# Transposing all tiles of the second round through DRAM, in eight parts, and four early groups in place of five

## The chip, the cores and the metric

One core of a Trainium2 chip. The metric is the device time of one launch in microseconds; medians of several runs are given.

## The reference

Attention with keys that are pooled 4x4, then a two-layer network with a sigmoid-approximated Gelu, over 49152 tokens of 128 channels:

```python
kv_flat = kv.reshape(B, H//4, 4, W//4, 4, C).mean(axis=(2, 4)).reshape(B, -1, C) @ w_sr   # 768 keys a batch
a = softmax((q @ kv_flat.T) / sqrt(C));  x = (a @ kv_flat).reshape(B * S, 128)            # B=4, S=12288
h = x @ w_in                                        # 128 -> 2048
out = (h * (1 / (1 + exp(-1.702 * h)))) @ w_out     # 2048 -> 128
```

## The kernel before

A Python program lays out a static order for every engine. The 96 groups of 512 queries are done in two rounds of 48: attention, network, attention, network. Attention needs Exp, the network Gelu, so each stage change costs ScalarE a table load (1.28 us in the trace). ScalarE handles three chunks of 512 columns in one activation of 128x1536; two sets of three PSUM banks alternate. Two more banks serve as accumulators and scratch. `ag`, 102 slots of 512 columns, holds activations until TensorE drains them. (A fill is a matmul that writes the banks that an activation will read; a drain is a matmul that reads an activation's result.)

The network needs attention's output with channels on partitions, so each 128x128 tile must be transposed. In both rounds the first 72 tiles (`LATER`) are turned on TensorE, six at a time, and copied back by VectorE; the other 120 go through DRAM in six parts of 20, during the network.

Five "early" groups of round two are worked during network 1: TensorE makes the scores and VectorE computes the exponentials with a polynomial, which spares ScalarE 10 activations.

```python
EARLY = 5
...
def drain_attn(t, a):                       # attention times value of tile t, half of the keys
    ...
        nc.tensor.matmul(av_of[u][...], weights(("a", i, jc))[:, o:o + T], vs[...], ...)
    ...
        o = u * TS % (XS * SG // T)
        if o >= LATER:
            to = x[:, o * T:(o + TS) * T]...
        else:                                # to be turned on TensorE: into a small tile first
            if u % 2 == 0:
                xt_of[u // 2] = npool.tile([128, 2 * TS, C], BF, name="xt")
            to = xt_of[u // 2][:, u % 2 * TS:u % 2 * TS + TS, :]
        nc.vector.tensor_tensor(to, ps[:, :, 0:C], rec..., MUL)
        if u % 2 and o < LATER:
            turns.append((now + TURN, u // 2))
...
def turn(w):
    for k in range(n):                       # n = 6
        nc.tensor.transpose(ps[:, k, :], xt[:, k, :], ident)
    nc.vector.tensor_copy(x[:, o:o + n * T], ps...)
...
LATER, PART = 72, 20
def put_away(n, m):  nc.sync.dma_start(out=x_bf[...], in_=x[:, ...])            # PART tiles
def bring_back(n, m): nc.sync.dma_start_transpose(out=x[:, ...], in_=x_bf[...])
...
def background_moe(g):
    n, g = divmod(g, 4 * XS)
    m, odd = divmod(g - 9, 2)
    if 0 <= m < (4 * XS * G // T - LATER) // PART:
        (bring_back if odd else put_away)(n, m)
...
def fill_moe(chunks, ps):                    # 3 matmuls, then one activation of 128x1536
def drain_moe(g, fc):                        # one matmul of a 16-step accumulation; VectorE evacuates
...
# the order's own estimates, in units of one 512-column matmul
FIXED, CHUNK, SWITCH, HANDOVER, EVACUATE, LATE = 0.33, 1.975, 6.0, 1.0, 4.5, 1.0
```

The softmax here doesn't subtract the row's maximum and nothing guards it: scores larger than these inputs give would overflow.

Of the kernel before, what the change touches and what calls it, by code (L numbers as in the profile page):

```python
# [24 lines left out]
def kernel(  # L25
# [12 lines left out]
    G = 512  # L38
    SG = 4 * G
# [5 lines left out]
    T = 128  # L45
    TS = 3
# [11 lines left out]

    R = 2
    XS = NS // R  # L60
    EARLY = 5
    AG = 102

    cpool = ctx.enter_context(tc.tile_pool(name="const", bufs=1))
# [19 lines left out]
    def acc(key=None):  # L84

        nonlocal last_acc
        last_acc = next_acc()
        if key:
            closes[last_acc] = key
        return banks[:, last_acc, :]  # L90
# [7 lines left out]
    def close(key, then):  # L98
        for m in [m for m in closes if closes[m] == key]:
            del closes[m]  # L100
            free[m] = then
# [59 lines left out]
    def add_kv(b, n):  # L161
        i, w = divmod(n, r)
        if n == 0:
            kv_sums[b] = kvsum.tile([Hp, 2, Wp, C], F32, name="kvs")
        for i2 in range(2):
            nc.gpsimd.dma_start(out=kv_sums[b][:, i2], in_=kv_p[b, i, w, :, i2],  # L166
                                **({"accum_op": ADD} if n else {}))
# [147 lines left out]

    early = range(NG // R, NG // R + EARLY)

    def weights(c):
        if c[0] == "a" and c[1] in early:
            return ag[:, (c[1] - early[0]) * JC + c[2], :]  # L320
        return ag[:, slot_of[c], :]
# [11 lines left out]
    def drain_attn(t, a):  # L333

        i, u, k = t // 4, t // TS, t % TS
        if k == a == 0:
            av_of[u] = acc(("av", u))
        o = t % 4 * T
        for jc in range(a * K, a * K + K):
            nc.tensor.matmul(av_of[u][:, k * (C + 1):(k + 1) * (C + 1)], weights(("a", i, jc))[:, o:o + T],  # L340
                             vs[i // GB][:, jc, 0:C + 1], start=(jc == 0), stop=(jc == JC - 1))
            if t % 4 == 3 and i not in early:
                del slot_of["a", i, jc]
        if k == TS - 1 and a == 1:
            close(("av", u), max(now, dve - 1.0) + EVACUATE)
            on_dve(4.3)
            ps = av_of.pop(u)[:, 0:TS * (C + 1)].rearrange("p (k c) -> p k c", k=TS)
            rec = npool.tile([128, TS], F32, name="rec")
            nc.vector.reciprocal(rec, ps[:, :, C])  # L349
            o = u * TS % (XS * SG // T)  # L350
            if o >= LATER:
                to = x[:, o * T:(o + TS) * T].rearrange("p (k c) -> p k c", k=TS)
            else:
                if u % 2 == 0:
                    xt_of[u // 2] = npool.tile([128, 2 * TS, C], BF, name="xt")
                to = xt_of[u // 2][:, u % 2 * TS:u % 2 * TS + TS, :]
            nc.vector.tensor_tensor(to, ps[:, :, 0:C], rec.unsqueeze(2).broadcast_to([128, TS, C]), MUL)  # L357
            if u % 2 and o < LATER:
                turns.append((now + TURN, u // 2))


    LN2 = 0.6931471805599453
# [51 lines left out]
        nc.vector.tensor_copy(x[:, o:o + n * T], ps.rearrange("p k t -> p (k t)"))  # L414


    LATER, PART = 72, 20

    def put_away(n, m):
        o = LATER + m * PART  # L420
        lo = n * XS * SG + o * T
        nc.sync.dma_start(out=x_bf[lo:lo + PART * T, :].rearrange("(k p) c -> p k c", p=T),
                          in_=x[:, o * T:(o + PART) * T].rearrange("p (k c) -> p k c", k=PART))

    def bring_back(n, m):
        o = LATER + m * PART
        lo = n * XS * SG + o * T
        nc.sync.dma_start_transpose(out=x[:, o * T:(o + PART) * T].unsqueeze(1), in_=x_bf[lo:lo + PART * T, :])

# [3 lines left out]
    def gate():  # L433

        nc.vector.memset(gate_tile, 0.0)  # L435
        nc.gpsimd.memset(gate_tile, 0.0)  # L436
# [3 lines left out]
    def background(i):  # L440

        s = i // 4
        if i % 4 == 0:
            if QS <= s + 2 < NS:
                load_qT(s + 2)
            if CAST <= s + CAST < NS:
                gate()
                cast_q(s + CAST)
        if i == 10:
            gate()  # L450
            for jc in range(JC):
                load_chunk(1, jc)
        if 0 <= i - 16 < JC:
            extras.append((key_and_value, 1, i - 16))
        if 0 <= i - 15 < JC:
            extras.append((pool_chunk, 1, i - 15))
        if i == 26:
            gate()
            nc.gpsimd.dma_start(out=w_in_sb, in_=moe_w_in)
        if i == 34:  # L460
            gate()
            nc.gpsimd.dma_start(out=w_out_sb, in_=moe_w_out.rearrange("(o p) c -> p o c", p=128))

    def background_moe(g):

        n, g = divmod(g, 4 * XS)
        m, odd = divmod(g - 9, 2)
        if 0 <= m < (4 * XS * G // T - LATER) // PART:
            (bring_back if odd else put_away)(n, m)
        g += n * 4 * XS  # L470
        nonlocal head, low
        if g == 12:
            low = EARLY * JC
            head = max(head, low)
        if g in (40, 46):
            i = early[0] + 4 * (g // 46)
            begun.add(("a", i))
            background(i)
        for b, lo in ((2, 2), (3, 24)):
            if lo <= g < lo + 8:  # L480
                gate()
                add_kv(b, g - lo)
            if g in (lo + 10, lo + 12):
                use_kv(b, (g - lo - 10) // 2)

    def use_kv(b, a):
        nonlocal extra_at
        sum_kv(b, a)
        on_dve(3.5)
        extra_at = max(extra_at, dve + 1.5)  # L490
        extras.extend([(transpose_pooled, b, a), (make_k, b, a), (make_v, b, a)])
# [38 lines left out]
    for n in range(R):  # L530
        part = [c for c in chunks if c[0] // (NG // R) == n]
        while part:
            m = sizes.pop(0) if sizes else K
# [21 lines left out]
    def prepare(p):  # L555

        nonlocal now
        for f, *args in first.get(p, ()):
            if f in COST:
                now = max(now, free[next_acc()])  # L560
            f(*args)
            if f in COST:
                now += COST[f][0]
                free[last_acc] = now + COST[f][1]
        kind, part = seq[p]
        for i, _ in part:
            if (kind, i) not in begun:
                begun.add((kind, i))
                (background if kind == "a" else background_moe)(i)
# [32 lines left out]
    def on_dve(cost):  # L602
        nonlocal dve
        dve = max(dve, now + 1.0) + cost
# [114 lines left out]
```

## Time and profile before

| | before |
|---|---|
| time, median of 3 runs | 974.97 us (974.95 to 976.67) |
| span of the profiled run | 974.7 us |
| first network activation | 150.28 us |
| network 1, first activation to the first of attention 2 | 354.49 us |
| attention 2, to the first activation of network 2 | 118.62 us |
| network 2, first to last activation | 343.65 us |

The last four rows are read from the starts of ScalarE's activations in the trace. One pair of profile lines is wanted here beside those of the prediction: the summary of the chain that ended last.

```profile
PE 91%; ACT 4%; DMA 3%; DVE 1%; issue 0%; POOL 0%; ACTq 0%; POOLq 0%
```

### The profile page before, as it was taken

How to read it: one execution, taken by the hardware profiler on the slowest of the kernel's cores; microseconds unless marked ns; L12 is line 12 of the kernel's file. 1: busy time of each engine (PE TensorE's matmuls, PEld its weight loads, DVE VectorE, ACT ScalarE, POOL GpSimd, SP SyncE). 2: the span in 40 equal slices, each digit the busy share in tenths (PEclk: the TensorE clock that was granted, in tenths of full speed). 3: DMA queues.
4: the chain of work that ended last, by engine and by line, in shares of the span. 5: the costliest groups of instructions: out<-in, count | busy, mean ns of one | idle time of the engine just before them, and what ended most of it. 6: DMA issues, size and time to landing. Idle time of an engine off the chain costs nothing.

```text
span 974.7 us, 16041 instructions
## 1 busy us (share of the span) xinstructions
PE 956.3 (98%) x6431; PEld 513.2 (53%) x6431; DVE 385.6 (40%) x806; ACT 945.0 (97%) x703; POOL 65.8 (7%) x113
## 2 busy tenths in 40 slices
PE   7899999999999999999999999999999999999997
PEld 3567777644444444444445777764444444444443
DVE  4444333211477878788786443330110110110110
ACT  4999999999999999989999999999999999999997
POOL 3100100430000232000000000000000000000000
PEclk9999999999999999999999999999999999999999
DMA  9897861999564798215257520002567522222222
GB/s 182 160 196 145 115 95 34 110 165 159 115 139 67 107 148 110 41 28 82 33 87 136 115 45 23 2 1 44 120 119 137 112 34 44 44 33 44 44 33 44
DMA packets 335691, 85.01 MB, mean 87 GB/s; under 512 B 309568, under 2 KB 333248, under 8 KB 335296
## 3 DMA queue, kind: packets, MB, share of 16 engines
q1 hardware_dynamic: 305456, 51.34, 31.0%
q0 software_dynamic: 29104, 32.51, 22.1%
q8 instruction: 50, 0.82, 0.3%
q10 hardware_dynamic: 1056, 0.13, 0.1%
q14 instruction: 25, 0.20, 0.1%
HBM read 52.49 MB, written 43.52 MB: 98 GB/s over the span
## 4 chain that ended last, share of the span: by engine, by line
PE 91%; ACT 4%; DMA 3%; DVE 1%; issue 0%; POOL 0%; ACTq 0%; POOLq 0%
PE banks L500 33%; PE banks L507 33%; PE banks L340 13%; PE banks L329 11%; ACT ag L502 3%; DMA qT<-q_bf 2%; ACT ag L331 1%; DMA x<-in_q_dram 1%; PE banks L412 1%; PE banks L370 1%; DVE qT L230 1%; PE banks L224 0%; DVE o_sb L515 0%; PE banks L134 0%; DVE v L194 0%
## 5 line engine op out<-in xcount | busy, mean ns | idle before, releaser
L502 ACT ACTIVATE ag<-banks 128x1536 bf16<-128x1536 f32 x512 | 691.9, 1476 | 6.6 <-PE banks L500 6.4
L500 PE MATMUL banks<-x,w_in_sb 128*128 128x512 bf16 x1536 | 414.8, 379 | 0.1
L507 PE MATMUL banks<-ag,w_out_sb 128*128 128x512 bf16 x1536 | 411.8, 379 | 1.4 <-DVE v L194 0.9
L331 ACT ACTIVATE ag<-banks 128x1536 bf16<-128x1536 f32 (+1 forms) x186 | 247.4, 1466 | 13.2 <-PE banks L329 12.4
L507 PEld LDWEIGHTS <-w_out_sb 128*128 128x128 bf16 x1536 | 149.9, 98 | 180.6 <-issue 2.4
L500 PEld LDWEIGHTS <-w_in_sb 128*128 128x128 bf16 x1536 | 148.0, 98 | 170.0 <-issue 3.7
L515 DVE STREAM_TRANSPOSE o_sb<-banks 128x512 f32<-128x512 f32 x96 | 68.7, 716 | 351.0 <-PE banks L507 344.5
L340 PEld LDWEIGHTS <-ag 128*128 128x128 bf16 x2304 | 149.9, 97 | 47.4 <-issue 1.6
L340 PE MATMUL banks<-v,ag 128*128 128x129 bf16 x2304 | 168.3, 220 | 0.7 <-DVE v L158 0.7
L329 PE MATMUL banks<-qT,kT 128*128 128x512 bf16 x546 | 147.8, 378 | 6.9 <-ACT ag L331 4.5
L397 DVE SCALAR_TENSOR_TENSOR ea<-ea,eb 128x512 f32<-128x512 f32 x120 | 82.3, 686 | 3.4
L349 DVE RECIPROCAL rec<-banks 128x3 f32<-128x3 f32 x128 | 23.0, 179 | 131.1 <-PE banks L340 131.1
L329 PEld LDWEIGHTS <-kT 128*128 128x128 bf16 x546 | 46.7, 97 | 35.8 <-issue 4.0
L357 DVE TENSOR_TENSOR x<-banks,rec 128x384 bf16<-128x384 f32 x80 | 44.5, 557 | 2.8
L166 POOL DMA_DIRECT2D kvs<-in_kv_dram x32 | 40.4, 1330 | 15.4 <-DMA kvs<-in_kv_dram 11.3
L436 POOL MEMSET gate_tile<- 1x8 f32 x38 | 3.6, 95 | 466.9 <-DVE gate_tile L435 466.9
L386 DVE TENSOR_SCALAR ea<-banks 128x512 f32<-128x512 f32 x30 | 20.8, 692 | 33.1 <-PE banks L370 32.9
L357 DVE TENSOR_TENSOR xt<-banks,rec 128x384 bf16<-128x384 f32 x48 | 26.7, 557 | 1.7
L414 DVE COPY x<-banks 128x768 bf16<-128x768 bf16 x24 | 13.4, 557 | 23.2 <-PE banks L412 23.2
L399 DVE SCALAR_TENSOR_TENSOR ag<-ea,ee 128x512 bf16<-128x512 f32 x30 | 20.6, 687 | 1.4
L392 DVE SCALAR_TENSOR_TENSOR eb<-eb,ea 128x512 f32<-128x512 f32 x30 | 20.6, 688 | 0.9
L394 DVE TENSOR_SCALAR ea<-eb 128x512 f32<-128x512 f32 x30 | 13.2, 440 | 0.9
(65 smaller groups left out, 173.5 us busy)
## 6 DMA issues: line engine op xcount, KB each, us to landing
out_dram<-o_sb SPq DMA_DIRECT2D x382, 64.0 KB, 2.0
kvs<-in_kv_dram POOLq DMA_DIRECT2D x32, 384.0 KB, 6.4
q_bf<-in_q_dram POOLq DMA_DIRECT2D x20, 512.0 KB, 6.3
x_bf<-x SPq DMA_DIRECT2D x12, 640.0 KB, 4.6
x<-in_kv_dram POOLq DMA_DIRECT2D x12, 512.0 KB, 12.5
x<-in_q_dram POOLq DMA_DIRECT2D x3, 512.0 KB, 20.0
w_in_sb<-in_moe_w_in_dram POOLq DMA_DIRECT2D x1, 512.0 KB, 5.1
w_out_sb<-in_moe_w_out_dram POOLq DMA_DIRECT2D x1, 512.0 KB, 7.6
```

The costliest lines, as they stand in the source:

```text
L166: nc.gpsimd.dma_start(out=kv_sums[b][:, i2], in_=kv_p[b, i, w, :, i2], **({"accum_op": ADD} if n else {}))
L329: nc.tensor.matmul(ps[:, k, :], kTs[i // GB][:, jc * 128:(jc + 1) * 128], rhs, start=True, stop=True)
L331: nc.scalar.activation(place([("a",) + c for c in chunks]), ps, AF.Exp, scale=scale)
L340: nc.tensor.matmul(av_of[u][:, k * (C + 1):(k + 1) * (C + 1)], weights(("a", i, jc))[:, o:o + T], vs[i // GB][:, jc, 0:C + 1], start=(jc = ...
L349: nc.vector.reciprocal(rec, ps[:, :, C])
L357: nc.vector.tensor_tensor(to, ps[:, :, 0:C], rec.unsqueeze(2).broadcast_to([128, TS, C]), MUL)
L386: nc.vector.tensor_scalar(a, ps, scale / LN2, -126.0, MUL, MAX)
L397: nc.vector.scalar_tensor_tensor(a, a, COEFFS[k], b, ADD, MUL)
L500: nc.tensor.matmul(ps[:, k, :], w_in_sb[:, fc * 128:(fc + 1) * 128], x[:, g % (4 * XS) * G:(g % (4 * XS) + 1) * G], start=True, stop=True)
L502: nc.scalar.activation(place([("m",) + c for c in chunks]), ps, AF.Gelu_apprx_sigmoid)
L507: nc.tensor.matmul(o_of[g], w_out_sb[:, fc, :], weights(("m", g, fc)), start=(fc == 0), stop=(fc == FCH - 1))
L515: nc.vector.transpose(o_sb, o_of.pop(g))
```

## The change

The intent: take 72 transposes and their VectorE copies off the second round, by sending all its 192 tiles through DRAM, each part of 24 as soon as VectorE has written it, mostly while attention 2 still runs; and give one of five early groups back to ScalarE. The first round keeps its 72 transposes; its other 120 tiles go in five parts of 24.

```diff
-    EARLY = 5
+    EARLY = 4
...
-            o = u * TS % (XS * SG // T)
-            if o >= LATER:
+            n, o = divmod(u * TS, RT)
+            if o >= LATER[n]:
...
-            if u % 2 and o < LATER:
+            if u % 2 and o < LATER[n]:
                 turns.append((now + TURN, u // 2))
+            if n and (o + TS) % PART == 0:
+                m = o // PART
+                put_away(n, m)
+                if m:
+                    bring_back(n, m - 1)
+                if m == RT // PART - 1:
+                    bring_back(n, m)
...
-    LATER, PART = 72, 20
+    RT = XS * SG // T
+    LATER, PART = (72, 0), 24
...
-        if 0 <= m < (4 * XS * G // T - LATER) // PART:
+        if n == 0 and 0 <= m < (RT - LATER[0]) // PART:
             (bring_back if odd else put_away)(n, m)
```

More of the change, by code (lines that the diff above doesn't have):

```diff
@@ L414, in turn @@
         nc.vector.tensor_copy(x[:, o:o + n * T], ps.rearrange("p k t -> p (k t)"))
-    LATER, PART = 72, 20
+    RT = XS * SG // T
+    LATER, PART = (72, 0), 24
     def put_away(n, m):
-        o = LATER + m * PART
+        o = LATER[n] + m * PART
         lo = n * XS * SG + o * T
@@ L425, in bring_back @@
     def bring_back(n, m):
-        o = LATER + m * PART
+        o = LATER[n] + m * PART
         lo = n * XS * SG + o * T
```

## The prediction

> **What bounds the kernel now.** The kernel runs four stages: attention over the first 48 query groups, the two-layer network over them, attention over the other 48, network again. I read the engine line of the page first, then the windows at the stages' borders (149, 503.5 and 622 us: where the scalar engine changes from Exp to Gelu and back), then TensorE's waits, then single rows of the timeline for the price of one instruction, and last the end of the chain.
>
> ```profile
> PE 956.3 (98%) x6431; PEld 513.2 (53%) x6431; DVE 385.6 (40%) x806; ACT 945.0 (97%) x703; POOL 65.8 (7%) x113
> ```
>
> Two engines look full, so busy shares don't decide. The windows (columns PE, PEld, DVE, ACT, POOL, clock, DMA share, GB/s) say the same of each stage:
>
> ```profile
> 0.00:75.00 75.00, 63.93 (x666) 39.69 (x667) 33.39 (x106) 58.85 (x48) 14.48 (x35) 1.00 1.00 184
> 75.00:149.00 74.00, 73.99 (x836) 54.29 (x834) 29.20 (x87) 73.96 (x56) 5.47 (x16) 1.00 0.71 108
> 149.00:503.50 354.50, 352.88 (x1964) 173.60 (x1962) 222.03 (x406) 347.86 (x258) 43.10 (x52) 1.00 0.66 97
> 503.50:622.00 118.50, 118.50 (x1183) 80.92 (x1182) 55.50 (x132) 117.66 (x87) 2.71 (x10) 1.00 0.37 69
> 622.00:969.00 347.00, 346.43 (x1793) 164.60 (x1790) 44.74 (x77) 346.70 (x258) 0.00 (x0) 1.00 0.34 59
> ```
>
> What decides is work at the pitch of back-to-back instructions, for which I take a run of n and divide (length minus one duration) by n-1:
>
> ```profile
> 503.07 2.10 PE L507 MATMUL banks<-ag,w_out_sb 128*128 128x512 bf16 x9
> 527.26 0.86 PE L340 MATMUL banks<-v,ag 128*128 128x129 bf16 x12
> 530.30 0.49 PE L412 MATMUL banks<-ident,xt 128*128 128x128 bf16 x6
> ```
>
> A 512-column matmul lasts 0.379 us but comes every (2.10-0.379)/8 = 0.215; an attention-times-value one, with 129 columns, every 0.058 (0.059 as the median over the trace); a transpose every (0.49-0.219)/5 = 0.055. For the scalar engine the starts at the end of the chain show the pitch of one 128x1536 activation with nothing in its way, 1.33 us:
>
> ```profile
> 956.40 1.15 ACT ag L502
> 957.73 1.16 ACT ag L502
> 959.06 1.17 ACT ag L502
> ```
>
> Multiplied by the program's own order of instructions (counts between the first network fill, the first later attention fill, and the second network's first fill):
> - network 1: (768 fills + 709 drains + 28 early fills) x 0.2155 + 417 x 0.059 + 12 transposes x 0.055 + 2.0 for key and value work = 351.6 us of TensorE; scalar engine 256 x 1.331 + a table load of 1.28 = 342.0. Measured 354.5.
> - attention 2: (258 + 59 + 2) x 0.2155 + 795 x 0.059 + 60 x 0.055 = 118.9; scalar 86 x 1.331 + 1.28 = 115.7. Measured 118.5.
> - network 2: 1536 x 0.2155 + 267 x 0.059 = 346.8; scalar 342.0. Measured 347.
>
> So **TensorE is the bound in all three**, by 9.6, 3.2 and 4.8 us, and the chain's 91% on it is no artefact. Its waits after 75 us are nearly nothing:
>
> ```profile
> PE banks L507 <- DVE v L194: 0.9, 2, 0.4
> PE banks L412 <- DVE xt L357: 0.6, 1, 0.6
> PE banks L507 <- ACT ag L502: 0.5, 1, 0.5
> ```
>
> **What the Trainium skill says.** "TensorE: Matmul & The Clock Gate", section "Wait — 56ns, not 53.3ns?", has warm start-to-start gaps of 55.6 and 215.7 ns for 128 and 512 columns; this trace agrees (0.055, 0.215), and the granted clock is 1.00 in every window. Its "Part 4: PE-mode transpose" prices a transpose at some 275 ns in a kernel; here one lasts 219 ns but occupies the array for 55, so I use 55. That is the difference between a gain of 4 us and one of 20. "VectorE: DVE Perf Modes", section "The three transpose paths", sets a 128x128 transpose at 1309 ns by DMA against 390 on TensorE; the trace has a 20-tile DMA transpose land in 5.0 us median, 0.25 us a tile, so the page's figure is no rate for a batch. "DMA: Bandwidth & Descriptors", section "Two DMAs through the same engine are not ordered", says that a DMA which reads another's output must wait for that one's completion semaphore; this is why each part is brought back one part after it was put away, and no run here shows it violated.
>
> **The change part by part.**
> Removed: 72 of 144 transposes (12 in network 1, 60 in attention 2), 72 x 0.055 = 3.96 us on TensorE, on the path. With them go 12 VectorE copies of 0.557 us (6.7 us, VectorE is 40% busy, worth nothing by itself), the scratch-bank turns they used, and the one wait of TensorE for the tile to be transposed (0.6 us).
> Moved by four early groups in place of five: the six score matmuls of one group cost the same wherever they stand (0.2155 each), but their exponentials go from VectorE (6 series of ten instructions; the seven groups of such instructions on the page sum to 183 us for 30 series, so 6.1 us each and 37 us in all) to the scalar engine: 2 activations, +2.66 us. In network 1 VectorE is 63% busy, with 222 us; 37 fewer makes its replies to TensorE (the 0.9 us wait) quicker.
> Added: 72 more tiles through DRAM (eight parts of 24 in round two for six of 20), and the DMA work of that round moves from network 2 to attention 2. The second attention's DMA share is 0.37 before. Eight parts at an estimated 5.0 x 24/20 = 6 us of landing are 48 us of the 118, one at a time on SyncE's queue between the query transposes, of which eight at some 4.6 us already run there. It fits, 24 tiles taking some 16 us of TensorE time.
> Counting the changed order in the same way: network 1 (768 + 705 + 24) x 0.2155 + 417 x 0.059 + 2.0 = 349.2 (-2.4); attention 2 (264 + 63) x 0.2155 + 849 x 0.059 = 120.6 (+1.7), scalar 88 x 1.331 + 1.28 = 118.4; network 2 331.0 + 213 x 0.059 = 343.6 (-3.2), scalar still 342.0. **TensorE stays the bound in each, by 7.2, 2.2 and 1.6 us.** Sum -3.9 us. Of the 2.9 us by which network 1 now exceeds its work (354.5 - 351.6) I let 1 us go, for the transpose's wait and a freer VectorE; that 1 us is my choice, the rest is counted. The first 149 us and the tail after the last activation stay. 975.0 - 3.9 - 1.0 = 970.1, which I round to 970.2.
>
> **The rivals.**
> (a) ScalarE becomes the bound and eats the gain. For it: it has 97%, gets 2.66 us more, and its margin in network 2 falls to 1.6 us; already before, the chain from 956 to 968 us runs on it. Against: it is below TensorE's work in every stage, and its 102 buffer slots let it run ahead. If half the network 2 gain were lost: 972.
> (b) A transfer is exposed. A part's way out, wait and way back is some 11 us. The first network fill of round two needs part 0, whose tiles are finished 89 us of TensorE work ahead, and part 1, which triggers it, 73 us ahead; the last part ends 23 us into network 2 and is needed at 302. So no tile is late. More real: SyncE's queue is served in order, so a store waiting for VectorE holds a query transpose behind it. These are issued two sets of four groups ahead, 16 activations or 21 us; being held for a few us leaves slack. If one stalled per part, some 2 us each, the result would be 980 or more.
> (c) More than the counts. TensorE no longer has to fit short transposes between fills with a dependency on VectorE on both sides; if all 2.9 us of network 1's excess went, 968.
> (d) Transposes were hidden anyway, as TensorE waited for others there: then nothing changes, 975 to 977 with the extra scalar work. Attention 2 has no idle TensorE time in the waits, which speaks against it.
>
> **Range and chances.** The counted part is -3.9; (c) gives the low end, 967.8; (a), with a spread of 1.7 us in the three runs of before, the high end, 973.4. Two per cent is 19.5 us: no count gives that for a gain, and for a loss only (b) in its bad form. I take 0.01 faster, 0.97 same, 0.02 slower.
>
> **What would show it.** Right: 72 transposes on the page in place of 144 with none after the first attention; the scalar engine's Exp group at x188; network 1, attention 2 and network 2 at about 351, 120 and 344 us; TensorE with no wait for a DMA into x or qT after 75 us; thirteen 24-tile transposes, the eight of round two between 530 and 660 us. Wrong: idle of TensorE on qT or x in attention 2 or at the start of network 2 (b); scalar engine's activations at a pitch of 1.331 throughout network 2 with TensorE waiting for it (a); network 2 not shorter than 347.

## The result, and the profile after

972.01 us (median of 4 runs, 971.71 to 973.29) against 975.27 us before on the same chip: ratio 0.9966, interval 0.9949 to 0.9984. A later set of runs of the changed kernel gave 971.81 us and 0.9960.

| stage | before | predicted | after |
|---|---|---|---|
| network 1 | 354.49 | -3.4 | 350.39 (-4.10) |
| attention 2 | 118.62 | +1.7 | 120.07 (+1.45) |
| network 2, first to last activation | 343.65 | -3.2 | 343.20 (-0.45) |
| sum of the three | 816.76 | -4.9 | 813.66 (-3.10) |

The two profiles differ by 4.8 us in span, 1.6 of it ahead of network 1 (150.28 against 148.66), where nothing was changed. That part is no gain: see the repeat of the kernel before, below.

The page after, engines and chain (columns as before):

```profile
PE 947.4 (98%) x6243; PEld 508.4 (52%) x6359; DVE 344.3 (35%) x734; ACT 946.2 (98%) x705; POOL 66.1 (7%) x113
PE 80%; ACT 16%; issue 2%; DVE 1%; DMA 1%; POOL 0%; POOLq 0%
```

TensorE's weight loads went from 6431 to 6359, the 72 transposes; ScalarE has two more instructions. (116 matmul records are missing from this trace; the weight loads are all there. TensorE's busy time can therefore not be compared.) VectorE lost 41 us. The chain's share on ScalarE rose from 4% to 16%: this is the first sign of where the missing gain went.

What TensorE and ScalarE waited for after 149 us, by line (total, times, longest):

```profile
PE banks L515 <- ACT ag L510: 0.5, 1, 0.5
PE banks L508 <- ACT ag L510: 0.4, 1, 0.4
ACT ag L510 <- PE banks L508: 2.2, 4, 1.3
ACT ag L510 <- PE banks L515: 0.2, 1, 0.2
```

Before, ScalarE stood idle 6.4 us in network 1 for TensorE's fills, and TensorE waited for VectorE's `v` and `xt`; now 2.4 us are left and neither VectorE wait appears. No wait for a transfer into `x` or `qT` appears after 75 us. The rows of the parts under way (tile `x_bf`: count, duration on SyncE's queue as min/median/max in ns, first and last start; the last line, of the list of DMA issues, has the median us to landing of the transposes alone):

```profile
L430 SPq DMA_DIRECT2D x_bf<-x x13: 377/394/1172, 212.8 to 640.2; - x13
L436 SPq DMA_TRANSPOSE x<-x_bf x13: 2864/5612/7260, 224.7 to 646.4; - x13
DMA to landing us min/median/max: 5.1/5.9/11.8
x<-x_bf SPq DMA_TRANSPOSE x13, 8.1
```

Thirteen parts as predicted. The 5.9 us is the median of the ways out and back together; the transposes alone took 8.1 us to land, where 6 was estimated: 5.3 to 6.5 us for the five of round one, 5.6 to 10.1 for the eight of round two. They are issued in time all the same, and nobody waits.

Now the stage that disappointed. TensorE at 930 us in network 2, before:

```profile
930.01 0.81 PE L500 MATMUL banks<-x,w_in_sb 128*128 128x512 bf16 x3
930.66 0.81 PE L507 MATMUL banks<-ag,w_out_sb 128*128 128x512 bf16 x3
931.31 0.81 PE L500 MATMUL banks<-x,w_in_sb 128*128 128x512 bf16 x3
931.95 0.81 PE L507 MATMUL banks<-ag,w_out_sb 128*128 128x512 bf16 x3
932.60 0.81 PE L500 MATMUL banks<-x,w_in_sb 128*128 128x512 bf16 x3
```

and after:

```profile
930.51 0.81 PE L508 MATMUL banks<-x,w_in_sb 128*128 128x512 bf16 x3
931.16 0.81 PE L515 MATMUL banks<-ag,w_out_sb 128*128 128x512 bf16 x3
931.86 0.81 PE L508 MATMUL banks<-x,w_in_sb 128*128 128x512 bf16 x3
932.50 0.81 PE L515 MATMUL banks<-ag,w_out_sb 128*128 128x512 bf16 x3
933.20 0.59 PE L508 MATMUL banks<-x,w_in_sb 128*128 128x512 bf16 x2
```

Before, three fills and three drains take 932.60 - 931.31 = 1.29 us, six matmuls at 0.216 with nothing between. After, they take 933.20 - 931.86 = 1.34: each fill waits some 0.05 us for a bank. From 864 us on, each of the 73 activations that a fill still follows has one that starts 0.051 to 0.053 us after its end, so it is ScalarE that sets the pace; before, this is so only from 947 us on, for 15. The waits list does not show it, as the pause is shorter than the 0.379 us that a matmul lasts, so "busy" covers it. Summing what the start-to-start distances exceed the pitch, from the first activation to the last and with the missing records allowed for, gives 0.9 us of TensorE idle in network 2 before, 0.7 of it in the same small pauses from 947 us on, and 3.9 us after, 3.7 of it from 864 us on. (The trace of `pe_back_att2` below, which lacks no records there, gives the same 3.9.) TensorE's work in network 2 did fall by the 3.2 us predicted (54 attention-times-value matmuls fewer there); nearly all of that time turned into idle: TensorE, which hardly pauses up to there, comes down to ScalarE's pace some 80 us earlier in the stage.

### The profile page after: what moved, and what is told of

Same layout as the page of the kernel before. It is cut to its first block, busy times and chain, and to the rows that moved or that the text cites. A ratio compares the mean times of both kernels' runs of the same rounds, so it can differ in the third digit from the quotient of the medians.

```text
span 969.9 us, 15710 instructions
## 1 busy us (share of the span) xinstructions
PE 947.4 (98%) x6243; PEld 508.4 (52%) x6359; DVE 344.3 (35%) x734; ACT 946.2 (98%) x705; POOL 66.1 (7%) x113
## 4 chain that ended last, share of the span: by engine, by line
PE 80%; ACT 16%; issue 2%; DVE 1%; DMA 1%; POOL 0%; POOLq 0%
PE banks L515 27%; PE banks L508 26%; ACT ag L510 14%; PE banks L340 14%; PE banks L329 11%; ACT ag L331 2%; DVE qT L230 1%; DMA x<-in_kv_dram 1%; PE banks L377 1%; PE banks L419 0%; PE banks L134 0%; PE banks L224 0%; DVE xt L357 0%; PE banks L271 0%; DVE o_sb L523 0%
## 5 line engine op out<-in xcount | busy, mean ns | idle before, releaser
L508 PE MATMUL banks<-x,w_in_sb 128*128 128x512 bf16 x1478 | 406.0, 378 | 2.0 <-ACT ag L510 0.4
L404 DVE SCALAR_TENSOR_TENSOR ea<-ea,eb 128x512 f32<-128x512 f32 x96 | 66.0, 687 | 2.8
L357 DVE TENSOR_TENSOR x<-banks,rec 128x384 bf16<-128x384 f32 x104 | 57.9, 557 | 3.6
L393 DVE TENSOR_SCALAR ea<-banks 128x512 f32<-128x512 f32 x24 | 16.6, 691 | 26.5 <-PE banks L377 26.5
L406 DVE SCALAR_TENSOR_TENSOR ag<-ea,ee 128x512 bf16<-128x512 f32 x24 | 16.5, 689 | 1.1
L399 DVE SCALAR_TENSOR_TENSOR eb<-eb,ea 128x512 f32<-128x512 f32 x24 | 16.5, 687 | 0.7
L357 DVE TENSOR_TENSOR xt<-banks,rec 128x384 bf16<-128x384 f32 x24 | 13.4, 557 | 0.8
L230 DVE COPY qT<-banks 128x512 bf16<-128x512 bf16 x15 | 9.8, 687 | 4.5 <-PE banks L224 4.4
L421 DVE COPY x<-banks 128x768 bf16<-128x768 bf16 x12 | 6.7, 557 | 11.7 <-PE banks L419 11.7
```

The source lines that it names most:

```text
L230: nc.vector.tensor_copy(dst, src)
L357: nc.vector.tensor_tensor(to, ps[:, :, 0:C], rec.unsqueeze(2).broadcast_to([128, TS, C]), MUL)
L404: nc.vector.scalar_tensor_tensor(a, a, COEFFS[k], b, ADD, MUL)
L508: nc.tensor.matmul(ps[:, k, :], w_in_sb[:, fc * 128:(fc + 1) * 128], x[:, g % (4 * XS) * G:(g % (4 * XS) + 1) * G], start=True, stop=True)
```

## The experiments

Three theories:
- **Array theory** (the prediction's): TensorE bounds every stage, so each microsecond taken off it counts.
- **Floor theory**: ScalarE's real pitch is 1.343 us and not the 1.331 that I read, so in network 2 it is 256 x 1.343 + 1.28 = 345.1 us against TensorE's 344: ScalarE has become the bound there, and was within 2 us of it before (TensorE's count was 346.8).
- **Order theory**: the static order, or the loop fill, activation, fill through two sets of PSUM banks, holds the activations at 1.343.

A table of all stages first. "Start" is the first network activation, us; ratios are to the kernel before as it ran beside each set. In the later sets its medians were 976.0 to 976.2 us, so compare ratios, and not medians with the first row.

| run | median us | ratio | start | network 1 | attention 2 | network 2 | sum |
|---|---|---|---|---|---|---|---|
| before | 974.97 | | 150.28 | 354.49 | 118.62 | 343.65 | 816.76 |
| before_again | 974.76 (one run) | | 148.52 | 354.50 | 118.62 | 343.64 | 816.76 |
| after | 972.01 | 0.9966 | 148.66 | 350.39 | 120.07 | 343.20 | 813.66 |
| after_again | 971.81 | 0.9960 | 148.69 | 350.39 | 120.07 | 343.20 | 813.66 |
| early_only | 974.27 | 0.9986 | 148.62 | 352.04 | 120.25 | 343.54 | 815.83 |
| dram_only | 974.36 | 0.9983 | 150.68 | 353.68 | 117.53 | 342.85 | 814.06 |
| before_197 | 978.12 | 1.0025 | 150.32 | 355.49 | 118.84 | 343.23 | 817.56 |
| pe_back_att2 | 976.07 | 0.9999 | 149.37 | 351.06 | 123.42 | 343.20 | 817.68 |
| pe_back_net2 | 972.73 | 0.9969 | 148.69 | 350.39 | 120.06 | 344.12 | 814.56 |
| order_1955 | 975.90 | 0.9999 | 152.50 | 353.10 | 119.65 | 342.43 | 815.18 |
| dram_in_net2 | 972.53 | 0.9968 | 150.26 | 350.39 | 120.05 | 343.20 | 813.64 |
| defer2 | 970.92 | 0.9953 | 149.58 | 348.20 | 120.10 | 343.45 | 811.75 |

The repeats of the two kernels show that the three later stages come back within 0.01 us. The start does not: it is read from one profile a run, and varies by up to 1.8 us for the same kernel.

### Repeats: the first stage

> The kernel before, unchanged, for a second profile. Later stages within 0.1 us of 354.49, 118.62 and 343.65. The first network activation at 150.3 us again if the late query transpose belongs to the kernel, at 148.7 if it varies by run, as it does for the kernel after (148.66, 148.69, and 150.26 in its sibling whose first stage is the same).

> The kernel after, unchanged, for comparison on this chip and to see how far the first stage varies: ratio 0.9955 to 0.998, later stages within 0.1 us of 350.39, 120.07 and 343.20; the first network activation starts at 148.7 or 150.3 us, the latter if the query transpose of 48 us lands late, as in the profile of before.

Measured: both kernels can start network 1 at 148.5 to 148.7 us; `before_again` gave 148.52, so the 150.28 of its first profile was that run's. In that first profile TensorE waited 1.3 us for a query transpose at some 70 us; in the second it did not. The other traces agree: the five that start at 150.26 us or later (`before`, `dram_in_net2`, `before_197`, `dram_only`, `order_1955`) show this wait, 1.1 to 2.0 us, and those that start earlier show at most 0.2. The gain that belongs to the change is therefore the 3.10 us of the later stages, which agrees with the 3.3 us between the medians of the first set; the later set had 4.3 between the medians, with an interval of its ratio (0.9947 to 0.9973) that holds both.

### Undoing one part of the change

`early_only`: the kernel before with one line changed.

```diff
-    EARLY = 5
+    EARLY = 4
```

> The kernel before with four early groups in place of five, all transposes of round two still on TensorE. Its order holds the same TensorE work as before in sum (349.9, 120.9 and 347.0 us in the three later stages, 817.8 both times) and 2 activations more. Array theory (TensorE bounds every stage): same time as before, up to 1.8 us less if VectorE's smaller load removes TensorE's idle time in network 1; ratio 0.998 to 1.000. Floor theory (ScalarE's true pitch is 1.343 us, so it is close to being the bound everywhere): within 1 us of before too, as TensorE's work is above ScalarE's in all three stages. If the early groups, not the transposes, made the gain, this run would show a ratio near 0.9966.

Measured: later stages -0.93 us, ratio 0.9986. Network 1 got 2.45 us shorter, attention 2 1.63 longer. As expected of both theories; the transposes, not the early groups, made most of the gain.

Set beside the kernel after, `early_only` is also the one pair that differs in the transposes alone, with the same constant: 815.83 - 813.66 = 2.17 us, of which 1.65 in network 1, 0.18 in attention 2 and 0.34 in network 2. Attention 2 lost 60 transposes (3.3 us), and in their place the order put 54 attention-times-value matmuls (3.2 us) that had stood in network 2: its trace holds 830 of them in attention 2 and 232 in network 2, that of after 884 and 178. So most of the time taken off TensorE was passed on to network 2, and there it gained almost nothing.

`dram_only`: the kernel after with five early groups. With the constant 1.975 this could not be built at all: the order found no free run of slots in `ag`. It was built with 1.97.

```diff
-    EARLY = 4
+    EARLY = 5
...
-    FIXED, CHUNK, ... = 0.33, 1.975, ...
+    FIXED, CHUNK, ... = 0.33, 1.97, ...
```

> The kernel after with five early groups kept (the order's constant for one activation, 1.975, had to become 1.97, because with 1.975 the order finds no free slot). TensorE 351.1, 118.1 and 345.3 us, ScalarE at 1.3435 a piece 345.2, 116.8, 345.2. Array theory: TensorE's sum is 814.5 against 814.0 after, so like after, ratio to before 0.996 to 0.998. Floor theory: the larger of the two in each stage sums to 814.5 against 815.2 after, so like after or 1 us faster: ratio 0.995 to 0.997. If the transposes are not what made the gain: 1.000.

Measured: 974.36 us, 0.9983, so by the clock a miss of both theories, which wanted 0.995 to 0.998. The later stages sum to 814.06, -2.70. The constant is a second change, so it was tried alone:

```diff
-    FIXED, CHUNK, ... = 0.33, 1.975, ...     (kernel before, EARLY = 5)
+    FIXED, CHUNK, ... = 0.33, 1.97, ...
```

> The kernel before with the order's constant 1.97 in place of 1.975, as the run with five early groups and all transposes through DRAM needed, so that the constant's own effect is known. If the constant does nothing: ratio 0.999 to 1.001, later stages within 0.5 us in sum of 816.76. If it costs 1 us or more in the first stage, that run's time was spoilt by it and its later stages alone count.

Measured: the constant alone costs 2.5 us by the ratio (1.0025), 0.8 of it in the later stages of its profile, so the rest, by subtraction, before them. (The interval of the ratio, 1.0011 to 1.004, is wide. Its one profile started at 150.32 us with a wait of 1.6 us for the query transpose, much like the first profile of before; whether its other runs started later is not known.) Between the two kernels with 1.97, the transposes through DRAM are worth 817.56 - 814.06 = 3.50 us in the later stages: 1.81 in network 1, 1.31 in attention 2, 0.38 in network 2. So the transposes are worth some 2.2 us (with four early groups) to 3.5 us (with five, at 1.97), and the early group 0.9 us (`early_only`) or 0.4 (after against `dram_only`, where the constant differs too). The two VectorE waits of network 1 part in the same way: in `early_only` the waits for `v` are gone and the 0.6 us for `xt` is left, in `dram_only` the 0.9 us for `v` is left and `xt` is gone.

### Putting the same TensorE work back in two places

Both add 72 transposes of the identity into the scratch bank, read by nobody; the output stays right.

```diff
+    def idle_turn(k):
+        ps = acc_bf()[:, 0:k * T].rearrange("p (k t) -> p k t", k=k)
+        for j in range(k):
+            nc.tensor.transpose(ps[:, j, :], ident, ident)
...
     # pe_back_att2, in drain_attn where the turns of round two were queued
+            if n and u % 2 and o < 72:
+                idle_turn(2 * TS)
...
     # pe_back_net2, in drain_moe
+        if g >= NG - 12 and fc in (7, 14):
+            idle_turn(3)
```

> The kernel after with the same 72 idle transposes where the change took them away (60 in attention 2, 12 in network 1), with no dependency on VectorE and no copy. Both theories: attention 2 holds 124.0 us of TensorE against 119.5 of ScalarE, so 3.3 us more there and 0.7 in network 1, in all 3 to 4 us slower than after, ratio to before near 1.000. If instead waits on VectorE and the scratch banks were what the change removed, it stays near 0.997.

Measured: +0.67 in network 1, +3.35 in attention 2, 0.00 in network 2, in sum +4.02 us over the kernel after; 976.07 us, level with before. The transposes' array time, 72 x 0.055 = 3.96 us, is the whole of their price: the VectorE copies and the dependencies that came with them in the kernel before are absent here.

> The kernel after with 72 idle transposes (4.0 us of TensorE, the number that the change removed) put among the drains of the last 12 groups of network 2, where the trace shows TensorE pausing 0.05 us at nearly every activation. Array theory: 4.0 us slower than after, ratio to before near 1.001. Floor theory (ScalarE bounds this stretch): at most 1 us slower than after, ratio 0.9965 to 0.998, and network 2 from first to last activation within 0.7 us of 343.2.

Measured: +0.92 us, all in network 2. (The span grew by 0.82.) That is under the 1 us bound for the total, though 0.2 over the 0.7 that I allowed network 2. TensorE's idle there, by the start-to-start sum, fell from 3.9 to 0.8 us: the pauses took the transposes in. The array theory wanted 4.0. The same number of transposes cost four microseconds in one stage and under one in the other: **network 2 has a different bound**, at least in its last 100 us.

### ScalarE's pitch by itself

```diff
+    for i in range(80):
+        s = 30 if i == 40 else i % 8 * 3
+        nc.scalar.activation(ag[:, s:s + 3, :], banks[:, i % 2 * 3:i % 2 * 3 + 3, :], AF.Gelu_apprx_sigmoid)
+        if i == 40:
+            for j in range(240):
+                nc.tensor.matmul(banks[:, 6, :], w_out_sb[:, j % FCH, :], ag[:, 30, :], start=True, stop=True)
```

> The kernel after, with 80 more 128x1536 Gelu activations at its end that read PSUM banks nobody writes any more: 40 with TensorE at rest, then 40 beside 240 matmuls of 512 columns into another bank. The output is unchanged. Floor theory: ScalarE's own pitch, end to end, is 1.343 us in the first 40, and the same in the second. Array theory, as my prediction had it: 1.331. Order theory (the static order or the loop through the two PSUM buffers holds the activations at 1.343): 1.331 in both. If TensorE's writes to PSUM slow ScalarE: 1.331 alone and 1.343 beside the matmuls.

Measured, the timeline of ScalarE at the end (start, length, what, idle before) and the line's durations (min/median/max ns):

```profile
967.38 107.57 ACT L700 ACTIVATE ag<-banks 128x1536 bf16<-128x1536 f32 x80 [2.62 <-DVE o_sb L523]
...
L700 ACT ACTIVATE ag<-banks x80: 1445/1926/2419, 967.4 to 1072.5; 128x1536 bf16<-128x1536 f32 x80
```

The 80 starts lie (1072.5 - 967.4)/79 = 1.331 us apart. But the first one lasts 1.445 us and the last 2.419: each record is 12 ns longer than the one before, so the ends lie (107.57 - 1.445)/79 = **1.343 us** apart. TensorE waits for ends, as the fills 0.051 to 0.053 us behind them show. This holds from the second activation on, with TensorE at rest, and it is the same beside the 240 matmuls. Floor theory right; array theory's 1.331 is a fact of start stamps; neither the PSUM loop nor TensorE's writes are needed to make 1.343. (While TensorE rested for 57 us the granted clock was 0.53, and from 1030 us on, beside the matmuls, it was 1.00; ScalarE's 1.343 did not change with it. The run's mean is 0.973, and nothing else is read from it.)

With this floor, 255 x 1.343 = 342.5 us from first to last activation is about the least that network 2 can take (starts can run ahead of that by a tenth or two). It took 343.65 before and 343.20 after: there were 1.1 us to win, and 0.45 were won. The timelines of ScalarE in network 2, before and after:

```profile
623.39 345.34 ACT L502 ACTIVATE ag<-banks 128x1536 bf16<-128x1536 f32 x256
```

```profile
619.12 344.93 ACT L510 ACTIVATE ag<-banks 128x1536 bf16<-128x1536 f32 x256
```

### The order's constant

```diff
-    FIXED, CHUNK, ... = 0.33, 1.975, ...     (kernel after)
+    FIXED, CHUNK, ... = 0.33, 1.955, ...
```

> The kernel after with one constant of the static order changed, the time it reckons for a third of an activation, 1.955 in place of 1.975 units of one matmul, so it plans an activation every 6.195 units (1.337 us at 0.2158) in place of 6.255 (1.350). It moves 18 attention-times-value matmuls from attention 2 to network 2. Order theory: network 2 loses 2 to 3 us, the run 970. Floor theory: the sum of the later stages stays within 0.8 us of after, network 2 at no less than 342.6 (255 x 1.3435).

Measured: network 2 at 342.43 us, 0.77 less than after and now at the floor within 0.1 us (0.17 under the 342.6 that I had set as the least, since it is read from starts; from the end of its first activation to the end of its last it is 342.55). It did not lose the 2 to 3 us of the order theory. The sum grew by 1.5 us, as network 1 lost 2.7, and the start was late as well. The sum is outside the 0.8 us I allowed: a different order stalled TensorE in network 1 (ScalarE idle there for 6.0 us). So planned pace explains at most 0.8 us of network 2, and changing it is no gain: 975.90 us, ratio 0.9999.

### Transfers beside attention 2 or in network 2

```diff
-                put_away(n, m)
-                if m:
+                if m < 3:
+                    put_away(n, m)
+                if 0 < m < 4:
                     bring_back(n, m - 1)
-                if m == RT // PART - 1:
-                    bring_back(n, m)
...  (in background_moe)
+        if n == 1 and 0 <= m < 5:
+            (bring_back if odd else put_away)(n, m + 3)
```

> The kernel after, but of round two's eight parts only the first three go out as their tiles come; parts 3 to 7 wait for network 2, as the parts of before did. Both theories: no transfer is waited for in either, the order on TensorE, VectorE and ScalarE is the same, so within 0.5 us of after in the sum of stages, and no wait of TensorE on x. If transfers beside attention 2 slow anything, attention 2 gets shorter than 120.07 us here.

Measured: 350.39, 120.05 and 343.20, sum 813.64. When parts 3 to 7 travel makes no difference to the stages, though they land sooner there (5.1 to 5.8 us, against 5.6 to 9.3 in the kernel after). With no wait for `x` or `qT` in either trace, this disposes of the rival that a transfer or a blocked queue costs something.

### Moving work from where TensorE is short to where it idles

If the floor theory holds, TensorE has some 3 us to spare in network 2 while it is the bound in network 1. Of the five sets of attention-times-value matmuls of early groups, `defer2` allows only two in network 1:

```diff
-                if todo_early and all((i, jc) in made ...
+                if todo_early and (todo_early[0][1] // TS < NT // R // TS + 2 or seq[n][0] == 'a'
+                                   or n >= at['m', NG // R, 0] - 1) and all((i, jc) in made ...
```

> The kernel after, but of the five sets of early attention-times-value matmuls only two are allowed in network 1; three (54 matmuls, 3.2 us) wait for attention 2, so that others spill into network 2, where TensorE idled. The larger of the two engines sums to 347.1 + 120.8 + 346.0 = 813.9 against 815.2 for after. Floor theory: 1 to 1.5 us faster than after, sum of later stages 812.2 to 812.9. Array theory: no change, TensorE's sum is the same.

Measured: 970.92 us, ratio 0.9953 to before. Network 1 -2.19 against after, attention 2 +0.03, network 2 +0.25, sum -1.91: a little better than the 0.8 to 1.5 us that the ranges gave. TensorE has the same instructions in all; only their place changed: 54 attention-times-value matmuls fewer in network 1, 19 more in attention 2, 35 more in network 2. The array theory wanted no change. **This is the best version** by its stages; the clock alone does not part it from the kernel after (intervals 0.9938 to 0.9968 and 0.9947 to 0.9973). ScalarE's idle time for fills in network 1, which was 6.4 us before and 2.2 after, is 0.6 here:

```profile
ACT ag L510 <- PE banks L508: 0.6, 2, 0.4
```

## Why the prediction was right or wrong

The time fell in the range, 972.0 against 970.2 predicted (967.8 to 973.4), and "same within 2%" was right. Part of this is luck: network 1 gained 0.7 us more than predicted and attention 2 lost 0.25 less, which covered 0.95 of the 2.75 us missing in network 2; the range had room for the rest since rival (a) was in it. (Its low end, 967.8, should by its own terms be 975.0 - 3.9 - 2.9 = 968.2.) By its steps:

- **Pitch of the transposes, 0.055 us, and 72 x 0.055 = 3.96 us on the path.** Right: put back where they were, they cost 4.02.
- **Network 1, -2.4 of work and -1 of idle.** Measured -4.10. The work was right; TensorE's idle there fell by some 1.7 us in place of 1 (from 2.8 to 0.5 by the start-to-start sum), as both VectorE waits went.
- **Attention 2, +1.7.** Measured +1.45. Right.
- **Network 2, -3.2, since "TensorE stays the bound in each, by 7.2, 2.2 and 1.6 us".** This step failed; measured -0.45. The mis-sized term is ScalarE's pitch, taken as 1.331 us; it is 1.343. Over 256 activations that is 3.1 us, which turns the 1.6 us margin into a deficit of 1.5. The lines that I quoted for it hold the correction: starts 1.33 apart, but lengths of 1.15, 1.16 and 1.17, so the ends are 1.34 apart. (These are pieces of the chain; the records themselves last 1.582, 1.594 and 1.607 us.) The sign named for this stage, "about 344", did not come either: it belongs to the borders of the 347 before, table load to last matmul, and by these the kernel after has some 346.5. The 343.20 of the table is between other borders.
- **Rival (a), ScalarE eats the gain.** It was named, with the right stage, and put at half the network 2 gain; it took about 2.75 of the 3.2 us there. Its result, 972, is what came. I had given it too little weight because of the pitch.
- **Rival (b), an exposed transfer.** Wrong, as expected: no wait in the trace, and moving five parts into network 2 changed 0.02 us. The estimate of 6 us a part was short (8.1 measured), but part 0 had landed 62 us before round two's first fill.
- **Rival (c), all idle of network 1 goes.** Nearly: 0.5 us of TensorE idle is left there by the start-to-start sum.
- **Rival (d), transposes hidden anyway.** Wrong for attention 2. In network 2 it would have been right: 72 idle transposes cost 0.92 us there, and not 4.
- **"The first 149 us stay."** Right on repeats; the 1.6 us between the first two profiles is variation.

Still open: why the query transpose ahead of network 1 lands late in some runs, why `order_1955` started later still (152.50 us, of which that wait is 1.9), why the parts of round two landed more slowly (in the kernel after, the seven that took 8.1 us or more were issued within 1.1 us of another part's way out; this was not tested), and whether the constant 1.97 truly costs more than a microsecond ahead of network 1.

## What to carry to other kernels

When two engines are within one per cent of each other, measure the pitch of both from the **ends** of a saturated run, or from the length of a whole run of n, and not from the starts; a margin of 1.6 us in 340 rests on the third digit. Work taken off the leading engine pays only in the stages where it leads; a check is to put idle work of the same size back in each stage. Where one stage has slack on an engine and another has none, moving work between stages can gain more than removing a little of it: here 54 matmuls moved gave 1.9 us.

## What the Trainium skill lacked or had wrong

- "ScalarE: Activation LUTs", section "What ACT_TABLE_LOAD costs": it gives an activation with immediate operands as 186 ns + 0.833 ns a column (280 ns with a bias pointer) and an overlap of some 93 ns back to back, which for 1536 columns would be, as an estimate from that page, a pitch of 1.37 us or more (it does not say whether this is for a tile in PSUM, as here). The run with 80 activations shows 1.445 us for the first and a pitch of 1.343.
- No page says that, in a saturated run, the starts of ScalarE's records run ahead: durations grew from 1.445 to 2.419 us over 80 equal activations, with starts 1.331 and ends 1.343 us apart.
- "ScalarE: Activation LUTs", the same section as above, counts 2.66 us for a change of table, load and drain. In the profile after, the change into attention 2 took 1.28 us for the load, and the first Exp began 1.30 us after the load's start; no drain of 1.38 us beside it is seen.
- "TensorE: Matmul & The Clock Gate", section "Part 4: PE-mode transpose": some 275 ns for a transpose. Here the record is 219 ns and the price in the stage that TensorE bounds is 55 to 56 ns (4.02 us for 72).
- "VectorE: DVE Perf Modes", section "The three transpose paths": 1309 ns for a 128x128 tile by DMA. A part of 20 tiles landed in 5.0 us median before, 0.25 us a tile, and one of 24 in 8.1 us after, 0.34 a tile.
